# One pair of v products held over from a group's short phase, and four small edits beside it

## The chip, the core and the metric

The kernel runs on one core of a Trainium2 chip. The metric is the device time of one execution in microseconds. A core has five engines that run their own instruction streams and meet at semaphores: TensorE (PE in the profile, its weight loads PEld), VectorE (DVE), ScalarE (ACT), GpSimd (POOL) and SyncE (SP), whose queue issues nearly all the DMAs of this kernel. On-chip data lies in SBUF (128 partitions); TensorE writes to PSUM.

## The reference

The input x has 2048 tokens of 512 features. Two branches see it and a gate mixes them:

```
g = sigmoid((x * gate_w).sum(-1))
q, k, v = split(x @ wqkv)            # 32 heads of 16 features
a = concat_heads(softmax(q k^T / 4) v) @ wo
h = layernorm(x)
u = gelu(h^T w1 + b1)                # over the tokens: 2048 -> 1792
b = (u w2 + b2)^T                    # 1792 -> 2048
out = g * a + (1 - g) * b
```

All is float32. b1 has 1792 values, b2 has 2048.

## The kernel before

Most float32 products are made of three products of split operands: `split` makes a high part (a cast) and a low part (source minus high part), and high x high, high x low and low x high are added. A cast is usually done on ScalarE (or DVE), the subtraction on GpSimd or DVE.

**Stage 1, v.** For each of 16 tiles of 128 tokens, `turn` transposes x (four 128x128 products with the identity, line 184), splits it, and the v columns are projected (line 73). `gate_dot` makes the gate's sum on DVE. A scheduler orders this stage, the next and the first layer.

**Stage 2, q and k.** Transposed q and k are projected, split and stored in DRAM. On the way the greatest absolute values of q and k are kept; `most` holds, for each of the 512 features, the product of the two greatest values. Summed over the 16 features of a head it bounds that head's scores. `least_shifts` compares the 32 sums with a limit and leaves a count in `flag`. At the end of the kernel a general path runs if the count is not zero; here it is zero. Before the change this test is two tiny products on TensorE (lines 338 and 342), with DVE between them, at the first block of the first layer. The layer norm of the first half of the rows lies in this stage.

**Stage 3, the first layer of the token MLP** (line 357). Blocks of w1, 128 tokens by up to 512 columns, are loaded up to four ahead, split on ScalarE and GpSimd, and multiplied with the layer norm rows: twelve steps of 128x128 by 512 for a full block. The second half of the layer norm rows is made meanwhile. `gelu` follows on DVE and ScalarE. `biases` loads b1 and b2 with a row for every 128 values, and turns them with two small products (line 378), after the second block.

**Stage 4, attention with the second layer beside it.** From here on each engine's order is the program's. There are 32 groups: a pair of heads, and half of the queries (1024). A group has eleven phases. Each of ten full phases issues six score products (line 700; the two heads use the two halves of TensorE's rows), and beside them up to six dense steps on the free half of the rows (line 738): the second layer of the MLP, or the output projection. Each two scores fill a `[128, 2, 512]` PSUM tile (`s`, three of them), and one exponential on ScalarE (line 709) makes a `pt` tile in SBUF (six of them). The eleventh phase is short: four scores and nothing beside. After a phase's scores stand the products with v (line 665) of the phase *before* it, so that ScalarE has time: `late` holds the units of one phase, and `apply_v` takes them two at a time, a pair for the two query blocks. A pair is eight `av` matmuls. A full phase leaves three pairs, a short one two. After a group's last pair DVE copies `av` out (line 631), the numerators go to DRAM, and the denominators are inverted (line 644) and stored.

Dense steps of two neighbouring phases add to one PSUM bank, one half of the rows after the other. A tiny GpSimd memset of `token` (line 742) is the fence between them: it waits for the last dense step of one phase, and the first dense step of the next waits for it.

Before the first phase, 30 steps of the second layer run alone (line 685), and two of w2's blocks are split there, with the cast on DVE and the subtraction on GpSimd. While the groups run, `dense` says which steps stand beside which pair of phases, and `calls` says what else is issued there. `fetch_o` loads four head pairs' numerators and broadcast inverses from DRAM (the tiles `o_lo` and `o_sum`, lines 519 and 520) and puts a `divide` on the list of slow work for DVE (line 523), one item of which is issued per pair of phases. The output projection of the later queries takes what was divided. `open_end` frees the memory of the MLP and opens the pool `end`, in which the third fetch of the second half puts its tiles.

Of the kernel before, what the change touches and what calls it, by code (L numbers as in the profile page):

```python
# [9 lines left out]
F32 = mybir.dt.float32  # L10
# [11 lines left out]
P = 128  # L22
# [3 lines left out]
H = 32  # L26
# [32 lines left out]
def gated_mix(ctx: ExitStack, tc: tile.TileContext, a_x, a_wqkv, a_wo, b_w1, b_b1, b_w2, b_b2, gate_w, out):  # L59
# [3 lines left out]
    def split(hi, lo, src, copy, sub):  # L63

        copy(hi, src)  # L65
        sub(lo, src, hi.bitcast(F32), ALU.subtract)  # L66
# [10 lines left out]
    dram = ctx.enter_context(tc.tile_pool(name="dram", bufs=1, space=DRAM))  # L77
    qp_d = [dram.tile([3, P, S], F32, name=f"qp{b}") for b in range(ND)]
    kp_d = [dram.tile([2, P, S], F32, name=f"kp{b}") for b in range(ND)]

    ident = const.tile([P, P], F32, name="ident")
    make_identity(nc, ident)
    head_of = const.tile([P, P // DH], F32, name="head_of")
    nc.vector.tensor_reduce(head_of, ident.rearrange("p (h d) -> p h d", d=DH), axis=AX.X, op=ALU.add)
    ones = const.tile([P, 1], F32, name="ones")
    nc.vector.memset(ones, 1.0)
    b1 = const.tile([P, NF], F32, name="b1")
# [47 lines left out]

    def split_weight(copy=None):
        if loaded:
            raw = loaded.pop(0)
            hi = wk.tile([P, NB], F32R, name="w_hi")[:, : raw.shape[1]]
            lo = wk.tile([P, NB], F32R, name="w_lo")[:, : raw.shape[1]]  # L140
            split(hi, lo, raw, copy or nc.scalar.copy, nc.gpsimd.tensor_tensor)
            ready.append((hi, lo))
# [22 lines left out]
    with tc.tile_pool(name="vp", bufs=1, side="right") as pool:  # L165
# [22 lines left out]
        def gate_dot(t):  # L188
# [4 lines left out]
            tc.keep_in_program_order(dot)  # L193

        def v_pairs(t):
            cols = slice(t * P, (t + 1) * P)
            return [((xt_hi[:, k, cols], xt_lo[:, k, cols]), wv[k][1:]) for k in range(ND)]
# [29 lines left out]
        for t in range(1, NS):  # L227
            if t + 4 < NS:
                load(t + 4)
            if t + 1 < NS:  # L230
                turn(t + 1)
            if t in (8, 12):
                qk_w.append(wcols(qk_cols.pop(0)))
            if t >= 3:
                gate_dot(t - 3)
            ps = bank()
            products(ps, v_pairs(t))
            v_out(t, ps)
# [94 lines left out]
    xt_ctx.close()  # L333

    def least_shifts():

        ps = bank()
        nc.tensor.matmul(ps[: P // DH, :ND], head_of, most, start=True, stop=True)
        far = bd.tile([P // DH, ND], F32, name="far")
        nc.vector.tensor_scalar(far, ps[: P // DH, :ND], BOUND_LIMIT, None, ALU.is_gt)  # L340
        pf = bank()[:1, :ND]
        nc.tensor.matmul(pf, ones[: P // DH, :], far, start=True, stop=True)
        ff = bd.tile([1, 1], F32, name="ff")
        nc.vector.tensor_reduce(ff, pf, axis=AX.X, op=ALU.add)
        nc.vector.tensor_copy(flag, ff)
# [13 lines left out]
    with tc.tile_pool(name="ln1", bufs=3, side="right") as ln, tc.tile_pool(name="gl", bufs=2, side="right") as gl:  # L359
# [12 lines left out]

        def biases():
            for src, dst, rows, mul in ((b_b1, b1, NF, 1.0), (b_b2, b2x2, NS, 2.0)):
                t = ln.tile([NS, P], F32, name="bias", bufs=2)[:rows]
                nc.sync.dma_start(t, src.rearrange("(r c) -> r c", c=P))
                pt = bank()[:, :rows]
                nc.tensor.transpose(pt, t, ident[:rows, :rows])
                nc.vector.tensor_scalar_mul(dst, pt, mul)

        for f0, cs in order.items():
            n = min(NB, F - f0) // P
            ps = [bank() for _ in range(n)]
            for c in cs:
                if f0 == 0 and c < NH:
                    ln_load(ln, NH + c)
                    ln_scale(ln, NH + c, 1)
                    ln_rows(ln, NH + c)
                hi, lo = weight()
                layer(ps, hi, lo, (h_hi[c], h_lo[c]), c == cs[0], c == cs[-1])  # L390
                if f0 == 0 and c == 0:
                    least_shifts()
                if f0 == 0 and c == 1:
                    biases()
            for i in range(n):
                gelu(ps[i], f0 // P + i)
# [219 lines left out]
    assert at == (NP + 12) * TWOS + 7  # L616
    call(at - 2, fetch_o, 1, 2)
    at = put_outputs(range(NH, NS - 3), 0, EARLY, at, [5, 4])
# [37 lines left out]

    def apply_v(g, units, last):

        for pair in zip(*([u for u in units if u[2] == qb] for qb in range(2))):
            for i, c, qb, pt in pair:  # L660

                added[qb] += 1
                for h in range(2):
# [7 lines left out]
                    )  # L671
        if last:
            added[:] = 0, 0
            return evacuate(g)

    engines = {getattr(mybir.EngineType, name) for name in ("PE", "Activation", "DVE", "Pool", "SP")}
    with tc.manual_schedule(engines=engines):
        kt, qt = {0: load_k(0)}, {0: load_q(0)}
        late = open_s = fence = None
# [32 lines left out]
        for grp in range(NG):  # L712
            at = [0, 0]
            for ph in range(2 * TWOS + 1):
# [31 lines left out]
                if second:  # L746
# [144 lines left out]
```

## Time and profile before

| | us |
|---|---|
| median of 3 runs | 1333.93 |
| lowest and highest | 1333.09, 1336.63 |
| the profiled execution, its own time | 1335.31 |
| its span, first to last instruction | 1333.4 |
| stage 1 and 2 (v, q, k), to about | 145 |
| first layer, to about | 305 |
| second layer alone, to about | 312 |
| 32 groups of attention, to about | 1308 |

The mean granted clock of TensorE was 0.996. The profiled execution took 1.38 us more than the median of the runs.

In the profile, "L665" is line 665 of the kernel before. A line of a timeline has the start in us from the span's start, the duration in us, the engine, the line, the operation, what is written `<-` what is read, the shape, and how many instructions were merged; brackets hold the idle time of the engine before it and what ended it. A matmul's duration overlaps the next one's, so starts are to be compared, not durations. A line of the chain has start, duration, engine and line. A line of a group has busy us and mean ns, then the engine's idle time before those instructions.

### The profile page before, as it was taken

Reading aid. Unit: us, or ns where it says so; the run is one execution under the profiler, and the core shown is the slowest. Engines: PE = TensorE matmul, PEld = TensorE weight load, DVE = VectorE, ACT = ScalarE, POOL = GpSimd, SP = SyncE. Lnnn points to the kernel's source line nnn. Section 1 sums busy time; section 2 is a strip of 40 time slices with the busy share of each in tenths; the row PEclk is TensorE's granted clock in tenths of the full one; section 3 lists DMA queues with packets and bytes.
Section 4 is the critical chain, followed back from the end, with each engine's and each line's share of the span. In section 5 each row is a group of like instructions: output and inputs, shape, how many; then the busy total and the mean of one; then the engine's idle time right before and its main releaser. Section 6 shows DMA issues by size and latency. Waiting matters only on the chain.

```text
span 1333.4 us, 32411 instructions
## 1 busy us (share of the span) xinstructions
PE 1314.6 (99%) x13288; PEld 770.0 (58%) x13288; DVE 413.5 (31%) x625; ACT 1096.3 (82%) x1264; POOL 202.3 (15%) x468
## 2 busy tenths in 40 slices
PE   9999999999999999999999999999999999999996
PEld 6888778876555555555555555455554555545553
DVE  3596571454121111222322111222111222132324
ACT  3344343447999999999999999999999999999993
POOL 0210254443011011011000011000110110100001
PEclk9999999999999999999999999999999999999998
DMA  3587643327343333334555344545333334454511
GB/s 119 165 275 294 206 119 95 95 75 156 73 85 65 61 73 83 67 75 96 121 109 129 68 76 90 100 111 125 61 65 73 77 68 81 72 113 108 108 53 67
DMA packets 93240, 138.41 MB, mean 104 GB/s; under 512 B 14149, under 2 KB 53211, under 8 KB 90011
## 3 DMA queue, kind: packets, MB, share of 16 engines
q1 hardware_dynamic: 92650, 135.46, 42.7%
q8 instruction: 107, 1.75, 0.6%
q10 hardware_dynamic: 432, 0.79, 0.2%
q14 instruction: 51, 0.41, 0.1%
HBM read 99.63 MB, written 36.56 MB: 102 GB/s over the span
## 4 chain that ended last, share of the span: by engine, by line
PE 94%; ACT 2%; DMA 1%; DVE 1%; SPq 0%; issue 0%; POOL 0%; POOLq 0%; DVEq 0%; ACTq 0%
PE av L665 35%; PE s L700 26%; PE acc L357 12%; PE dn L738 11%; PE acc L73 10%; ACT pt L709 2%; DMA o_sum<-r 1%; PE dn L685 1%; PE acc L184 0%; DMA wv_raw<-in_A_wqkv_dram 0%; DVE sums L783 0%; SPq L419 0%; POOL w_lo L66 0%; DVE base L805 0%; DVE lo L66 0%
## 5 line engine op out<-in xcount | busy, mean ns | idle before, releaser
L709 ACT ACTIVATE pt<-s 128x1024 f32<-128x1024 f32 x1024 | 964.9, 1028 | 33.9 <-PE s L700 26.6
L700 PE MATMUL s<-qs,ks 64*128 64x512 f32 x2048 | 527.4, 421 | 3.0 <-ACT pt L709 3.0
L665 PE MATMUL av<-pt,v 128*17 128x256 f32 x8192 | 510.6, 381 | 0.0
L700 PEld LDWEIGHTS s<-qs,ks 64*128 64x128 f32 x2048 | 301.0, 184 | 207.8 <-ACT pt L709 155.4
L665 PEld LDWEIGHTS av<-pt,v 128*17 128x17 f32 x8192 | 205.2, 97 | 259.6 <-issue 125.3
L738 PE MATMUL dn<-u_hi,w_hi 64*128 64x512 f32 x428 | 182.3, 426 | 0.7 <-POOL token L742 0.7
L66 POOL TENSOR_TENSOR w_lo<-w_raw,w_hi 128x512 fp32r<-128x512 f32 (+1 forms) x128 | 154.4, 1209 | 136.5 <-ACT w_hi L65 111.4
L738 PE MATMUL dn<-u_lo,w_hi 64*128 64x512 f32 x428 | 169.6, 396 | 0.0
L738 PE MATMUL dn<-u_hi,w_lo 64*128 64x512 f32 x428 | 168.4, 393 | 0.0
L742 POOL MEMSET token<- 1x1 f32 x320 | 29.3, 92 | 875.8 <-PE dn L738 552.2
L631 DVE COPY ot<-av 128x512 f32<-128x512 f32 x32 | 22.1, 692 | 352.9 <-PE av L665 347.5
L644 DVE RECIPROCAL rt<-rt 128x512 f32<-128x512 f32 x31 | 103.9, 3353 | 1.1
L65 ACT CAST w_hi<-w_raw 128x512 fp32r<-128x512 f32 (+1 forms) x67 | 37.8, 566 | 65.9 <-PE acc L357 59.9
L357 PE MATMUL acc<-h_hi,w_lo 128*128 128x512 f32 x224 | 89.2, 398 | 0.3 <-POOL w_lo L66 0.3
L357 PE MATMUL acc<-h_hi,w_hi 128*128 128x512 f32 x224 | 89.0, 397 | 0.0
L357 PE MATMUL acc<-h_lo,w_hi 128*128 128x512 f32 x224 | 88.8, 396 | 0.0
L738 PEld LDWEIGHTS dn<-u_lo,w_hi 64*128 64x128 f32 x428 | 79.2, 185 | 3.4
L738 PEld LDWEIGHTS dn<-u_hi,w_lo 64*128 64x128 f32 x428 | 79.0, 185 | 3.6
L738 PEld LDWEIGHTS dn<-u_hi,w_hi 64*128 64x128 f32 x428 | 78.7, 184 | 3.7 <-POOL token L742 1.0
L65 DVE CAST w_hi<-w_raw 128x512 fp32r<-128x512 f32 (+1 forms) x61 | 22.4, 378 | 124.4 <-PE dn L738 66.8
L434 DVE TENSOR_SCALAR row<-dn,b2x,omg 128x512 f32<-128x512 f32 x16 | 13.0, 810 | 147.8 <-PE dn L738 106.5
L73 PE MATMUL acc<-xt_hi,wc_hi 128*128 128x512 f32 x128 | 49.8, 389 | 0.0
(131 smaller groups left out, 1065.8 us busy)
## 6 DMA issues: line engine op xcount, KB each, us to landing
w_raw<-in_B_w_dram SPq DMA_DIRECT2D x96, 256.0 KB
ks<-kp SPq DMA_DIRECT2D x192, 128.0 KB
qs<-qp SPq DMA_DIRECT2D x256, 64.0 KB
qp<-pc SPq DMA_DIRECT2D x16, 768.0 KB
x<-in_A_x_dram SPq DMA_DIRECT2D x32, 256.0 KB
kp<-pc SPq DMA_DIRECT2D x16, 512.0 KB
w_raw<-in_B_w_dram SPq DMA_DIRECT2D x32, 128.0 KB
bp<-row SPq DMA_DIRECT2D x16, 256.0 KB
```

Of the source, the lines that this page charges most:

```text
L65: copy(hi, src)
L66: sub(lo, src, hi.bitcast(F32), ALU.subtract)
L73: nc.tensor.matmul(ps, a, b, start=start and n == 0, stop=stop and n == last)
L357: nc.tensor.matmul(p, a, b, start=first and k == 0, stop=last and k == 2)
L631: nc.vector.tensor_copy(ot, av)
L644: nc.vector.reciprocal(rt, rt)
L665: nc.tensor.matmul(av[32 * j : 32 * j + VC, i * QC : (i + 1) * QC], v[:, c, g % NP * 2 + i, :], pt[:, h * QC : (h + 1) * QC], start=added[ ...
L685: nc.tensor.matmul(ps, a, b, start=start, stop=stop)
L700: nc.tensor.matmul(s[:, m, :], kt[grp][rows, c * P : (c + 1) * P], qt[grp][rows, qb * NB : (qb + 1) * NB], start=True, stop=True,)
L709: nc.scalar.activation(pt, s, AF.Exp, scale=SCALE)
L738: mm = nc.tensor.matmul(ps, a[half], b[half], start=first and not second, stop=last and bool(second))
L742: fence = nc.gpsimd.memset(token, 0.0)
```

## The change

Five edits:

1. **A pair held over.** `late` becomes a list of pairs. Behind the scores of a group's short phase only two of the three pairs of the last full phase are issued; the third is issued behind the next phase's six scores, ahead of the short phase's two. The last group keeps the old order.
2. **Test of the shifts on DVE.** `most` is stored to DRAM and read back as one row of 512 on one partition (`bring_most`, after the first block of the first layer); at the ninth block DVE sums it by heads, compares, counts. The two products on TensorE and their two constants go. The scheduler places the DVE part among the layer norm's work, before the rows of the ninth block.
3. **Biases turned with x.** The two bias tiles are cleared on GpSimd to 128x128, loaded in stage 1 after the sixth x tile, and turned as full tiles directly after x tile 5.
4. **First splits on DVE.** The two weight blocks split beside the 30 lone steps have their subtraction on DVE.
5. **A fetch one step earlier.** The third fetch of the second half is issued one pair of phases earlier, in the same step as `open_end`.

```diff
+    most_d = dram.tile([P, ND], F32, name="most_d")
...
-    head_of = const.tile([P, P // DH], F32, name="head_of")
-    nc.vector.tensor_reduce(head_of, ident.rearrange("p (h d) -> p h d", d=DH), axis=AX.X, op=ALU.add)
-    ones = const.tile([P, 1], F32, name="ones")
-    nc.vector.memset(ones, 1.0)
...
-    def split_weight(copy=None):
+    def split_weight(copy=None, sub=None):
...
-            split(hi, lo, raw, copy or nc.scalar.copy, nc.gpsimd.tensor_tensor)
+            split(hi, lo, raw, copy or nc.scalar.copy, sub or nc.gpsimd.tensor_tensor)
...
+        def biases(pool):
+            for n, (src, dst, rows, mul) in enumerate(((b_b1, b1, NF, 1.0), (b_b2, b2x2, NS, 2.0))):
+                t = pool.tile([P, P], F32, name=f"bias{n}")
+                nc.gpsimd.memset(t, 0.0)
+                nc.sync.dma_start(t[:rows], src.rearrange("(r c) -> r c", c=P))
+                pt = bank()[:, :P]
+                nc.tensor.transpose(pt, t, ident)
+                nc.vector.tensor_scalar_mul(dst, pt[:, :rows], mul)
...
+            if t == 4:
+                biases(pool)
...
+    most_row = bd.tile([1, P * ND], F32, name="most_row", bufs=1)
+    def bring_most():
+        nc.sync.dma_start(most_d, most)
+        nc.sync.dma_start(most_row, most_d.rearrange("p b -> (p b)")[None, :])
     def least_shifts():
-        ps = bank()
-        nc.tensor.matmul(ps[: P // DH, :ND], head_of, most, start=True, stop=True)
-        far = bd.tile([P // DH, ND], F32, name="far")
-        nc.vector.tensor_scalar(far, ps[: P // DH, :ND], BOUND_LIMIT, None, ALU.is_gt)
-        pf = bank()[:1, :ND]
-        nc.tensor.matmul(pf, ones[: P // DH, :], far, start=True, stop=True)
-        ff = bd.tile([1, 1], F32, name="ff")
-        nc.vector.tensor_reduce(ff, pf, axis=AX.X, op=ALU.add)
+        far = bd.tile([1, H], F32, name="far", bufs=1)
+        heads = far.rearrange("o (h b) -> o h b", b=ND)
+        nc.vector.tensor_reduce(heads, most_row.rearrange("o (h d b) -> o h b d", d=DH, b=ND), axis=AX.X, op=ALU.add)
+        nc.vector.tensor_scalar(far, far, BOUND_LIMIT, None, ALU.is_gt)
+        ff = bd.tile([1, 1], F32, name="ff", bufs=1)
+        nc.vector.tensor_reduce(ff, far, axis=AX.X, op=ALU.add)
         nc.vector.tensor_copy(flag, ff)
...
                 if f0 == 0 and c == 0:
+                    bring_most()
+                if f0 == 0 and c == NH:
                     least_shifts()
-                if f0 == 0 and c == 1:
-                    biases()
...
-    call(at - 2, fetch_o, 1, 2)
+    call(at - 3, fetch_o, 1, 2)
...
-    def apply_v(g, units, last):
-        for pair in zip(*([u for u in units if u[2] == qb] for qb in range(2))):
+    def pairs_of(g, units, last):
+        pairs = list(zip(*([u for u in units if u[2] == qb] for qb in range(2))))
+        return [(g, pair, last and n == len(pairs) - 1) for n, pair in enumerate(pairs)]
+    def apply_v(pairs):
+        ot = None
+        for g, pair, last in pairs:
             for i, c, qb, pt in pair:
...
-                split_weight(nc.vector.tensor_copy)
+                split_weight(nc.vector.tensor_copy, nc.vector.tensor_tensor)
...
-                if late:
-                    apply_v(*late)
-                late = grp, units, ph == 2 * TWOS
-        last_ot = apply_v(*late)
+                n = 2 if ph == 2 * TWOS and grp < NG - 1 else len(late)
+                apply_v(late[:n])
+                late = late[n:] + pairs_of(grp, units, ph == 2 * TWOS)
+        last_ot = apply_v(late)
```

More of the change, by code (lines that the diff above doesn't have):

```diff
@@ L371, in gelu @@
             split(u_hi[:, fb, :], u_lo[:, fb, :], u, nc.scalar.copy, nc.vector.tensor_tensor)
[L373 to L379, printed above, removed]
         for f0, cs in order.items():
@@ L671, in apply_v @@
                     )
-        if last:
-            added[:] = 0, 0
-            return evacuate(g)
+            if last:
+                added[:] = 0, 0
+                ot = evacuate(g)
+        return ot
     engines = {getattr(mybir.EngineType, name) for name in ("PE", "Activation", "DVE", "Pool", "SP")}
@@ L678, in gated_mix @@
         kt, qt = {0: load_k(0)}, {0: load_q(0)}
-        late = open_s = fence = None
+        late, open_s, fence = [], None, None
         for n, (step, *args) in enumerate(first):
             if n and n % 12 == 0:
-                split_weight(nc.vector.tensor_copy)
+                split_weight(nc.vector.tensor_copy, nc.vector.tensor_tensor)
             ps, a, b, start, stop, done = step(*args)
```

## The prediction

> **What bounds the kernel now.** I read the page first, then the chain of waits in order of time, then the timelines of PE, PEld and ACT at the ends of two groups, and last the places where the chain leaves TensorE.
>
> ```profile
> PE 1314.6 (99%) x13288; PEld 770.0 (58%) x13288; DVE 413.5 (31%) x625; ACT 1096.3 (82%) x1264; POOL 202.3 (15%) x468
> PE 94%; ACT 2%; DMA 1%; DVE 1%; SPq 0%; issue 0%; POOL 0%; POOLq 0%; DVEq 0%; ACTq 0%
> L709 ACT ACTIVATE pt<-s 128x1024 f32<-128x1024 f32 x1024 | 964.9, 1028 | 33.9 <-PE s L700 26.6
> ```
>
> The chain is TensorE almost throughout. In attention (about 1000 us, 32 groups) ScalarE is close behind: 964.9 us of exponentials and 33.9 us of idleness, most of it waiting for scores. So a group has two limits, and the prediction is about the places where one of them waits for the other. A group has ten full phases (six scores, dense steps beside, three pairs of v products: 24 `av` matmuls) and a short phase of four scores. The end of the first group, whose next phases have six dense steps (PE, then PEld, then ACT):
>
> ```profile
> 342.64 1.49 PE L665 MATMUL av<-pt,v 128*17 128x256 f32 x24
> 344.06 0.50 PE L700 MATMUL s<-qs,ks 64*128 64x512 f32 x1
> 345.64 1.06 PE L665 MATMUL av<-pt,v 128*17 128x256 f32 x16
> 346.62 0.49 PE L700 MATMUL s<-qs,ks 64*128 64x512 f32 x1
> 348.46 1.49 PE L665 MATMUL av<-pt,v 128*17 128x256 f32 x24
> ...
> 347.79 0.18 PEld L700 LDWEIGHTS s<-qs,ks 64*128 64x128 f32 x1 [0.41 <-ACT pt L709]
> ...
> 337.72 6.79 ACT L709 ACTIVATE pt<-s 128x1024 f32<-128x1024 f32 x7
> 344.88 8.45 ACT L709 ACTIVATE pt<-s 128x1024 f32<-128x1024 f32 x9 [0.37 <-PE s L700]
> ```
>
> Behind the short phase's four scores stand the 24 v products of the full phase before it (342.64 to 344.06: 1.42 us), behind the next six scores only 16 (345.64 to 346.62: 0.98). So the six scores come late, ScalarE idles 0.37 us, and one phase later TensorE waits for ScalarE (347.79): a score needs the PSUM bank that the third exponential of the late run frees. An exponential takes 1.03 us and the next starts 0.93 after it ((8.45 - 1.03) / 8), so that one ends at 344.88 + 2 x 0.93 + 1.03 = 347.77. The phase from 346.62 to the end of the next v products (348.46 + 1.42 = 349.88) is 3.26 us long. Where nothing waits, such a phase takes 3.00 (first two lines below).
>
> ```profile
> 1228.08 1.49 PE L665 MATMUL av<-pt,v 128*17 128x256 f32 x24
> 1231.08 1.49 PE L665 MATMUL av<-pt,v 128*17 128x256 f32 x24
> 1235.74 1.49 PE L665 MATMUL av<-pt,v 128*17 128x256 f32 x24
> ...
> 1225.21 0.75 DVE L543 SCALAR_TENSOR_TENSOR row<-dn,g,row 128x512 f32<-128x512 f32 x1 [1.12 <-PE dn L738]
> ...
> 1210.45 0.42 SPq L539 DMA_DIRECT2D row<-bp  x1
> ...
> 1219.96 12.00 DMA o_sum<-r
> ```
>
> The third line is the one long hole of attention: the fetch of the divisors lands 12.00 us after its issue, the divide on DVE comes behind it, and the phase lasts 4.66 us.
>
> **Held pair.** The work of TensorE is the same; one of three pairs (8 matmuls, 1.42 / 3 = 0.47 us by the 24, 0.44 by the difference 1.42 - 0.98) moves from behind the short phase's scores to behind the next six. At the boundary above: the six scores start at 343.62 and not 344.06; their first exponential is ready 0.82 later as now, at 344.44, when ScalarE is just free (337.72 + 6.79 = 344.51, less the overlap of 0.10). The third exponential ends at 347.33, before the score that waits until 347.79. The v products then take 1.42, so the next phase still begins at 346.62, and it is 3.00 long: 0.26 won. I take 0.25; the low end is half of it, 0.13, should a new wait in the first of the two phases take the rest.
>
> The other kind has four dense steps in the next phases, and there ScalarE is the limit:
>
> ```profile
> 404.88 1.49 PE L665 MATMUL av<-pt,v 128*17 128x256 f32 x24
> 406.30 0.50 PE L700 MATMUL s<-qs,ks 64*128 64x512 f32 x2
> 407.12 0.39 PE L700 MATMUL s<-qs,ks 64*128 64x512 f32 x1
> 408.67 0.75 PE L700 MATMUL s<-qs,ks 64*128 64x512 f32 x3
> 409.84 0.49 PE L700 MATMUL s<-qs,ks 64*128 64x512 f32 x1 [0.19 <-ACT pt L709]
> ...
> 400.14 6.62 ACT L709 ACTIVATE pt<-s 128x1024 f32<-128x1024 f32 x7
> 406.93 10.31 ACT L709 ACTIVATE pt<-s 128x1024 f32<-128x1024 f32 x11 [0.17 <-PE s L700]
> ```
>
> ScalarE's last exponential ends at 406.76, so it began at 405.73 and the next could begin at 406.66; it begins at 406.93: 0.27 lost. After the change the scores start at 405.86, the first exponential is ready at 406.49, and that loss goes. What is late next: the fifth score (407.12, 0.82 after the first) comes at 406.68, but its bank is freed by the exponential that ends at 406.76. TensorE waits 0.1 and loses 0.1 more in restarting, and the longer v products follow; the next phase begins at 408.87 instead of 408.67, its first exponential is ready 0.63 later, at 409.50, and ScalarE is free at 409.45. Net 0.22 won. The wait may be as long as the 0.19 seen at 409.84, so I take 0.15, between ends of 0 and 0.27.
>
> How many of each? Only at the second kind does the chain go through two exponentials; there are 14 such pieces, the first and the last of them:
>
> ```profile
> 407.85 1.95 ACT pt L709 x2
> 1249.61 1.95 ACT pt L709 x2
> ```
>
> A fifteenth, near 1217, is hidden by the fetch. So 15 x 0.15 + 16 x 0.25 = 2.25 + 4.0 = 6.25 us; ends 16 x 0.13 = 2.1 and 16 x 0.26 + 15 x 0.27 = 8.2. The held pair keeps one more `pt` buffer in use. That buffer is wanted again by the first exponential of the phase after, near 409.5, and its v products now come first in the run that starts near 407.5, so I cost it at nothing; had they come last it would still be 0.6 early.
>
> **Fetch one step earlier.** Its two DMAs are issued behind the `row` load of 1210.45, thus near 1211, and land by about 1225 if they again take some 2 and 12 us. The divide keeps its place on DVE, behind the instruction of 1225.21, and then runs with no wait: it can start at 1225.96, where now it waits until 1231.96. On SP the store of a partial row, eight `qs` loads and a `row` load are moved behind it, by the issue of two DMAs; the first scores that need the `qs` are 30 us away. Won: 4.66 less an undisturbed phase, which is 3.00 or, with ScalarE as the limit, 3 x 0.93 = 2.8; so 1.66 to 1.86, and I take 1.8.
>
> **Test of the shifts, biases.** Four tiny edits leave TensorE, which is gapless there:
>
> ```profile
> 145.36 0.40 PE L357 MATMUL acc<-h_hi,w_hi 128*128 128x512 f32 x1
> 148.63 0.40 PE L357 MATMUL acc<-h_hi,w_lo 128*128 128x512 f32 x1
> 150.21 0.39 PE L357 MATMUL acc<-h_hi,w_hi 128*128 128x512 f32 x1
> 156.30 0.40 PE L357 MATMUL acc<-h_hi,w_lo 128*128 128x512 f32 x1
> 157.95 0.40 PE L357 MATMUL acc<-h_hi,w_hi 128*128 128x512 f32 x1
> 19.87 0.60 PE L184 MATMUL acc<-ident,x 128*128 128x128 f32 x4
> 20.23 0.48 PE L73 MATMUL acc<-wv_hi,xt_hi 128*128 128x512 f32 x1
> ...
> L66 DVE TENSOR_TENSOR h_lo<-hf,h_hi x8: 676/684/693, 160.8 to 181.0; 128x512 fp32r<-128x512 f32 x8
> ```
>
> Twenty-six steps from 150.21 to 156.30 are 0.234 each. The four steps from 148.63 to 150.21 hold the two products of the test: 1.58 - 0.94 = 0.64. The four from 156.30 to 157.95 hold the two bias turns: 1.65 - 0.94 = 0.71. Added are two turns of full 128x128 tiles right behind the four of an x tile, which take 0.36: 0.18 for two, at most 0.5 if each costs a switch as the old ones did. Net 1.35 - 0.18 = 1.17, low end 0.85. On SP two bias loads move to the start (their tiles are needed near 20 us), and two small DMAs through DRAM take their place; DVE waits for the second of these ahead of the layer norm rows. The nearest row for that reduction is one of 512 elements, 0.68; DVE gains about as much by the operations it drops. The eight rows are split between 160.8 and 181.7. They are wanted from eight blocks of twelve steps after the layer's start (145.36) to fifteen blocks after it, 168 to 188, so 6 us cover it.
>
> **First splits on DVE.**
>
> ```profile
> 313.57 1.27 POOL L66 TENSOR_TENSOR w_lo<-w_raw,w_hi 128x512 fp32r<-128x512 f32 x1 [1.62 <-PE dn L738]
> 314.77 0.09 POOL L742 MEMSET token<- 1x1 f32 x1
> ...
> 313.73 0.50 PE L700 MATMUL s<-qs,ks 64*128 64x512 f32 x1 [0.19 <-ACT pt L709]
> 314.92 0.50 PE L738 MATMUL dn<-u_hi,w_hi 64*128 64x512 f32 x1 [0.69 <-POOL token L742]
> ...
> 306.74 2.19 POOL L66 TENSOR_TENSOR w_lo<-w_raw,w_hi 128x512 fp32r<-128x512 f32 x1 [1.17 <-ACT w_hi L65]
> 307.70 1.52 DVE L367 TENSOR_SCALAR gs<-gs 128x512 f32<-128x512 f32 x1
> ```
>
> The first fence (`token`) stands behind a split of 1.27 us on POOL; TensorE waits from 313.73 to 314.92. With the split on DVE the fence is free at once. But the scores of that phase also wait for exponentials: the first bank frees near 313.7 (the 0.19 at 313.73), the third 2 x 0.93 later, near 315.55, and two scores behind it (0.33 each after a wait) bring the v products to 316.2. As it is they begin six steps after 314.92, 0.33 + 4 x 0.23 + 0.33 later, at 316.5. I take 0.3, ends 0 and 1.0.
> In the last two lines a POOL split of 2.19 us (1.27 alone) lies over a DVE instruction of 1.52. The Trainium skill ("SBUF — State Buffer", the section on the two separate sides) says that DVE and GpSimd lock a shared pair of ports against each other, and that a two-port DVE copy holds up any GpSimd instruction. By that rule the fence's memset can now stand behind the DVE cast instead, and this term is about 0; by the row it is 0.3. The sum would be 9.2 and not 9.5.
>
> **Sum.** 6.25 + 1.8 + 1.17 + 0.3 = 9.5 us, with the low ends together 4.6, with the high ends 12.2. The profiled execution took 1335.31 (span 1333.4), so its like would take 1325.8; the median of the runs is 1333.93, 1.4 lower, and gives 1324.4. The case's own range is 1321.7 to 1329.3. A difference under 0.3% (4 us) I count as no change.
>
> **Rivals.** (1) The wait only moves: in the changed kernel the fifth score stands still at every boundary, and what ScalarE wins is given back there. For it: the bank frees 0.08 us after the score comes. Against it: with six dense steps all six scores stand on one half of the rows, the fifth comes 0.33 + 3 x 0.23 after 343.62, at 344.64, and its bank is free at 344.51. Then the held pair gives nothing, and the rest 3.3: 1330.7, within 0.3%. (2) The fetch's stall stays, because the earlier transfer shares the DMA engines with the eight `qs` loads: 9.5 - 1.8 = 7.7, so 1326.2. Against it: for the whole stall to stay it would have to take some 18 us and not 12, and before, it ran beside `ks` loads. (3) Slower: DVE stands in the first layer behind the row of 512 sums, which goes to DRAM and back. The layer norm rows wait behind it on DVE, and on ScalarE square roots that wait for DVE stand ahead of the weight casts. From 6 us of delay TensorE loses one for one; the gain is gone at 15.5 us, and beyond 19.5 it is slower by over 0.3%. Two landings as long as the 12.00 above, one behind the other, would make 24 us and 1342. Against it: these two move 2 KB each.
>
> **Chances.** Forecast 0.74; (1) 0.12; (2) 0.07; (3) and anything like it 0.07. Faster is the forecast, (2) and a part of (1), less the low tail: 0.82. Same 0.12, slower 0.06. The range from 1320.5 to 1331 takes in (1) and (2).
>
> **What would show it.** `av` runs of 16 behind the four scores and 24 behind the six; ScalarE's idleness for scores at 26.6 us falling by several; no wait of PEld for ScalarE in the second phase of a group; the pieces of two exponentials gone from the chain; no `o_sum` piece in it; the layer's steps 0.234 throughout; the first fence right after its matmul. Wrong would be: a new wait of TensorE in the first phase of each group, or a gap in the first layer.

## The result and the profile after

The changed kernel takes 1328.61 us (median of 7 runs, 1328.09 to 1329.23); the kernel before, beside it, 1333.93. The ratio is 0.9954 with a 95% interval of 0.994 to 0.9968: faster by 5.3 us, where 9.5 were forecast. The profiled execution took 1328.09 us with a span of 1326.2, 7.2 less than the span before; of these, 1.4 are the distance of the profiled execution of before from its own median, and 0.5 that of the changed kernel's.

The page of the changed kernel, the same groups as before and two of the first layer (the last column is TensorE's or ScalarE's idle time just ahead of these instructions, and what ended most of it):

```profile
PE 1309.7 (99%) x13284; PEld 767.8 (58%) x13284; DVE 414.3 (31%) x626; ACT 1095.7 (83%) x1264; POOL 202.0 (15%) x468
PE 95%; DVE 2%; issue 1%; POOL 1%; ACT 0%; DMA 0%; SPq 0%; POOLq 0%; DVEq 0%
L720 ACT ACTIVATE pt<-s 128x1024 f32<-128x1024 f32 x1024 | 964.4, 1026 | 26.9 <-PE s L711 17.7
L370 PE MATMUL acc<-h_hi,w_lo 128*128 128x512 f32 x224 | 89.1, 398 | 1.9 <-POOL w_lo L66 1.8
L370 PE MATMUL acc<-h_hi,w_hi 128*128 128x512 f32 x224 | 88.7, 396 | 0.4 <-ACT w_hi L65 0.4
```

ScalarE and the long transfer have left the chain (2% and 1% before), and ScalarE's idleness for scores fell from 26.6 to 17.7 us. TensorE's own idleness for exponentials fell from 3.0 to 0.4 us. But TensorE now waits in the first layer, and POOL and DVE stand in the chain. The timelines of TensorE and ScalarE at the two boundaries that the prediction showed, and of TensorE and DVE at the fetch:

```profile
343.01 1.49 PE L675 MATMUL av<-pt,v 128*17 128x256 f32 x24
345.09 1.06 PE L675 MATMUL av<-pt,v 128*17 128x256 f32 x16
347.69 1.49 PE L675 MATMUL av<-pt,v 128*17 128x256 f32 x24
...
339.24 10.53 ACT L720 ACTIVATE pt<-s 128x1024 f32<-128x1024 f32 x11 [0.16 <-PE s L711]
...
406.94 1.06 PE L675 MATMUL av<-pt,v 128*17 128x256 f32 x16
409.53 1.49 PE L675 MATMUL av<-pt,v 128*17 128x256 f32 x24
...
398.49 19.67 ACT L720 ACTIVATE pt<-s 128x1024 f32<-128x1024 f32 x21 [0.17 <-PE s L711]
...
1224.10 1.49 PE L675 MATMUL av<-pt,v 128*17 128x256 f32 x24
1227.12 1.49 PE L675 MATMUL av<-pt,v 128*17 128x256 f32 x24
...
1222.14 1.22 DVE L528 TENSOR_TENSOR o_sum<-o_lo,o_sum 128x1024 f32<-128x1024 f32 x1
```

Sixteen products now stand behind the short phase's scores and 24 behind the next; ScalarE runs through both boundaries (one run of 11 exponentials, and one of 21 that only the end of the view cuts off); the long phase at the fetch is 3.02 us. Attention, from the first score to the first matmul of the tail, takes 990.68 us (314.60 to 1305.28) and took 999.51: 8.8 won, 8.35 forecast (held pair, fetch and first splits).

The loss lies ahead of attention. The first score starts at 314.60, before at 311.88: 2.7 later, where 1.2 earlier was forecast. The chain of waits of the changed kernel in the first layer (start, duration, what):

```profile
165.11 1.52 POOL w_lo L66
...
170.07 1.28 POOL w_lo L66
...
174.46 1.26 POOL w_lo L66
...
177.58 1.30 POOL w_lo L66
...
181.51 1.29 POOL w_lo L66
```

Five times the chain goes through the split of a weight. TensorE sits idle for the low halves of the last four (0.28, 0.62, 0.08 and 0.63 us) and once for a high half (0.42). And at the end of the layers (timelines of TensorE and DVE):

```profile
306.01 0.40 PE L370 MATMUL acc<-h_hi,w_lo 128*128 128x512 f32 x1
307.61 0.47 PE L696 MATMUL dn<-u_hi,w_hi 128*128 128x512 f32 x1 [1.20 <-ACT gs L379]
...
304.25 1.76 DVE L415 MEMSET ks<- 16x2048 f32 x1 [0.46 <-issue]
306.05 1.41 DVE L378 TENSOR_SCALAR gu<-acc,b 128x512 f32<-128x512 f32 x2
```

The first product of the lone second layer starts 1.60 us after the last one of the first layer, 1.37 more than a step. Before, it followed at 304.98 on 304.75. (The row names ScalarE's `gs`, which ends at 307.47; the second `gu` on DVE, the last to read the first layer's PSUM tiles, ends at 307.46.)

### The profile page after: what moved, and what is told of

It reads as the page before. It is cut to its first block, busy times and chain, and to the rows that moved or that the text cites. A ratio compares the mean times of both kernels' runs of the same rounds, so it can differ in the third digit from the quotient of the medians.

```text
span 1326.2 us, 32411 instructions
## 1 busy us (share of the span) xinstructions
PE 1309.7 (99%) x13284; PEld 767.8 (58%) x13284; DVE 414.3 (31%) x626; ACT 1095.7 (83%) x1264; POOL 202.0 (15%) x468
## 4 chain that ended last, share of the span: by engine, by line
PE 95%; DVE 2%; issue 1%; POOL 1%; ACT 0%; DMA 0%; SPq 0%; POOLq 0%; DVEq 0%
PE av L675 37%; PE s L711 28%; PE dn L749 10%; PE acc L73 10%; PE acc L370 9%; DVE ks L415 1%; PE dn L696 1%; PE acc L181 1%; POOL w_lo L66 1%; DMA wv_raw<-in_A_wqkv_dram 0%; DVE u_lo L66 0%; DVE sums L795 0%; DVE gs L381 0%; DVE gu L378 0%; ACT pt L720 0%
## 5 line engine op out<-in xcount | busy, mean ns | idle before, releaser
L720 ACT ACTIVATE pt<-s 128x1024 f32<-128x1024 f32 x1024 | 964.4, 1026 | 26.9 <-PE s L711 17.7
L370 PEld LDWEIGHTS acc<-h_hi,w_lo 128*128 128x128 f32 x224 | 42.1, 188 | 14.1 <-POOL w_lo L66 4.1
```

The source lines that it names most:

```text
L370: nc.tensor.matmul(p, a, b, start=first and k == 0, stop=last and k == 2)
L720: nc.scalar.activation(pt, s, AF.Exp, scale=SCALE)
```

## The experiments

Times are medians beside runs of the kernel before on the same chip. Because the start of an execution, up to the first layer, varies by up to 2 us (the layer's first matmul stood between 145.3 and 147.2 us in the traces), stages are compared by their lengths: "the layer" is from its first matmul to the first product of the second layer, 159.62 us before and 162.32 after.

**The two terms of attention, alone.** `held_only` is the kernel before with edit 1, `fetch_only` with edit 5, `splits_only` with edit 4 of the list above; their diffs are the parts of the change's.

> The kernel before, with the pair of units held over from a group's short phase as the only edit. Forecast of the prediction: 15 x 0.15 + 16 x 0.25 = 6.25 us faster than before, between 2.1 and 8.2, thus a ratio near 0.9953. If the wait only moved to the fifth score: 0. In the changed kernel attention as a whole is 8.8 us shorter, of which group 29, with the fetch, has 2.08, so the pair should give 6.0 to 6.7 here and the ScalarE idleness for scores should fall from 26.6 to about 18.

Measured: 1328.23 against 1334.24, ratio 0.9951 (0.9937 to 0.9964). Its page:

```profile
L715 ACT ACTIVATE pt<-s 128x1024 f32<-128x1024 f32 x1024 | 964.6, 1026 | 26.6 <-PE s L706 17.9
```

The exponentials of all groups but the one with the fetch take 957.97 us from first to last, before 964.34: 6.4 won.

> The kernel before, with the fetch of the divisors issued one step earlier as the only edit. Forecast of the prediction: 1.66 to 1.86 us faster (1.8 taken). Rival: the transfer shares the DMA engines with the qs loads and the stall stays: 0. In the changed kernel group 29 is 2.08 shorter, with the held pair's share in it, so 1.7 to 2.0 is likely; the hole of 4.66 us between two runs of 24 v products near 1231 should read 3.0.

Measured: 1333.18 against 1334.24, ratio 0.9991 (0.9982 to 1.0). In the trace the divide no longer waits, and the group with the fetch is 30.93 us long against 32.77: 1.84, as forecast. But that 32.77 belongs to one execution. In the four other traces in which the fetch stands at its old place it is 31.56 and 31.58 (`held_only`, `splits_only`), 30.92 and 31.70 (`trip_added`, `wide_trip`, below). Without the stall it is 30.93, or 30.67 with the held pair; so the stall was 1.84, 0.9, 0.65, 0 and 0.8 us, 0.8 in the mean. The medians differ by 1.1 us, with an interval that reaches to nothing.

> The kernel before with the first splits of attention (those of the eleven or so dense steps ahead of the first group) on DVE as the only edit. Forecast of the prediction: 0.3 us (0 to 1.0), by the rule of the shared ports about 0. In the changed kernel the first group is 0.45 us shorter than with the held pair alone (31.54 and 31.99), so 0.4 to 0.5 is likely, seen in the first fence and in group 0; the medians cannot tell that from 0.

The steps meant there are the 30 lone ones, beside which two weight blocks are split. Measured: 1333.63 against 1333.65, ratio 0.9998 (0.9989 to 1.0007), nothing that the medians can tell. The first group is 31.97 us, before 32.24: 0.27 won, and 0.45 beside the held pair (31.54 after 31.99). The fence and TensorE in its trace:

```profile
313.75 0.09 POOL L742 MEMSET token<- 1x1 f32 x1 [4.71 <-PE dn L738]
...
313.84 0.50 PE L700 MATMUL s<-qs,ks 64*128 64x512 f32 x1 [0.18 <-ACT pt L709]
313.89 0.50 PE L738 MATMUL dn<-u_hi,w_hi 64*128 64x512 f32 x1
```

The fence was at 314.77 and is at 313.75; TensorE waits for a bank instead, as the prediction worked out.

**The bank.** The 8 PSUM tiles named `acc` are drawn in turn. Without the two products of the test, two tiles fewer are drawn ahead of the layers, so the tile that `dn` takes at the end is now the very last one that the first layer filled, and DVE must read it first (`gu<-acc` at 306.05, behind a memset). `one_bank` lets both biases share a tile, which moves all later ones by one:

```diff
-                pt = bank()[:, :P]
+                if n == 0:
+                    both = bank()
+                pt = both[:, n * P : (n + 1) * P]
```

> The changed kernel, but the two turned biases share one PSUM tile, so one tile fewer is drawn from the rotation of eight and every later tile moves by one bank. Bank theory: the 1.2 to 1.4 us that TensorE waits ahead of the first dn product (307.61 in the changed kernel) come from the rotation alone, since the changed kernel's last two layer tiles sit in the banks that the dn product takes next; with the shift that wait is gone and the time falls by 1.2 to 1.4 us, to about 1327.3. Rival: the wait comes from a late DVE (four memsets of 1.76 us ahead of the last gelu); then the bank does not matter, the wait stays and the time is the changed kernel's, within 0.3 us. The gaps of the first layer (165 to 185 us) stay in both.

Measured: 1326.27 against 1334.24, ratio 0.9937 (0.9924 to 0.9951). TensorE at the same place:

```profile
306.78 0.39 PE L372 MATMUL acc<-h_hi,w_lo 128*128 128x512 f32 x1
307.01 0.39 PE L698 MATMUL dn<-u_hi,w_hi 128*128 128x512 f32 x1
```

The wait is gone, with the memsets and the last gelu where they were: the bank it was, 1.37 us. The layer is 2.5 us shorter than in the changed kernel; the other 1.1 are shorter waits for weights (table below).

**The test back on TensorE.** `test_on_pe` is the changed kernel with the old `least_shifts` and no trip through DRAM.

> The changed kernel with the test of the shifts put back on TensorE as in the kernel before: no trip through DRAM, two tiny products back (0.64 us), and the rotation of banks as before. Trip theory (the 16-byte packets and what stands behind them cost the 2.7 us of gaps in the first layer, and the missing two banks 1.2 to 1.4 at the entry of attention): 2.7 + 1.3 - 0.6 = 3.4 us faster than the changed kernel, with the steps of the first layer 0.234 throughout. Rival (the bias loads and the new order of ScalarE and DVE make the gaps): they stay, and it is only 1.3 - 0.6 = 0.7 us faster.

Measured: 1326.28 against 1334.24, ratio 0.994 (0.9926 to 0.9953), 2.3 below the changed kernel's median, between the two expectations; but in the trace the layer takes 158.60 us, without a gap. Against 159.62 before, the biases' turns alone give 1.0: 0.7 for the turns and 0.3 for the wait at 178.29, which is gone.

**The trip alone, and its packets.** In the changed kernel's trace the store's 128 packets of 16 bytes lay beside 2 KB packets that took 217 to 836 ns (means of half microseconds) instead of 88. `trip_added` is the kernel before with the two transfers, `wide_trip` stores 512 bytes a row instead (of another tile that is ready earlier, so the store is issued 0.7 us sooner):

```diff
+        nc.sync.dma_start(most_d, most)
+        nc.sync.dma_start(most_row, most_d.rearrange("p b -> (p b)")[None, :])
...
-        nc.sync.dma_start(most_d, most)
+        with tc.issue_after(last_qp[0].ins):
+            nc.sync.dma_start(most_d, ident)
```

> The kernel before with only the trip of the bounds through DRAM added (the store of 128 x 16 bytes and the load of the row of 512); nothing reads the row, the test stays on TensorE. Packet theory: in the changed kernel the store's 128 packets of 16 bytes made the 2 KB packets beside them take 217 to 836 ns each in place of 88, and the rows of x behind them landed 1.7 us later; here the same, with packets of that length at about 150 to 153 us, and gaps of TensorE in the first layer of 1 to 2.7 us: 1 to 2.7 us slower than before. Rival (the gaps come from DVE's reduction and the new places of the square roots): packets hardly longer, no gap, 0.

> As trip_added, with the store made of 128 packets of 512 bytes in place of 16 (another tile of 128 x 128 is stored, the load of 512 values reads four of its rows; nothing uses it). The order of every queue is that of trip_added. Packet theory (it is the 16 bytes that hold up the neighbours): the 2 KB packets beside the store stay near 88 ns, the rows of x land as in the kernel before, no gap, and the time is 1 to 2.7 us below trip_added. Rival (any store at this place does it, since it stands in the same queue): as trip_added, packets long and the gaps there.

Measured: 1337.30 and 1337.41 against 1333.94, ratios 1.0023 (1.0013 to 1.0033) and 1.0023 (1.0014 to 1.0032). The layer takes 162.67 and 162.27 us, 3.05 and 2.65 more than before. The page of the first (that of the second has the same figures):

```profile
L364 PE MATMUL acc<-h_hi,w_lo 128*128 128x512 f32 x224 | 89.5, 400 | 2.1 <-POOL w_lo L66 2.1
```

So the trip costs 3 us even where nothing reads its row, and with packets of either size. The slow 2 KB packets are in `wide_trip` too (346 ns in the half microsecond behind the store), and in the next kernel, which has no store at all (283 ns at the same place). So the size of the packets is not what `trip_added` pays for.

The size does show elsewhere: in how much the DMA queues move just behind the store, and in when the first row of x is asked for. Times are in us after the layer's first matmul; the rate is that of the 2 us from 5.5 to 7.5.

| kernel | store | GB/s | first load of x | first square root | second |
|---|---|---|---|---|---|
| before | none | 149 | 6.0 | 10.9 | 11.8 |
| trip_added | 128 x 16 bytes | 31 | 7.4 | 11.7 | 15.0 |
| wide_trip | 128 x 512 bytes | 154 | 6.0 | 10.2 | 14.7 |
| after | 128 x 16 bytes | 33 | 7.8 | 13.5 | 15.7 |
| no_trip | none | 173 | 5.9 | 11.4 | 12.1 |

The five kernels with the 16-byte store at this place move 31 to 49 GB/s there, the nine others 142 to 182. The first load of x waits on SyncE until a store of q has landed. That is 7.1 to 7.7 us after the layer's first matmul in those five, and 5.8 in the nine (the changed kernel's load, and SyncE's waits for q's store):

```profile
153.10 0.33 SPq L269 DMA_DIRECT2D x<-in_A_x_dram  x1
SPq L269 <- DMA qp<-pc: 2.5, 1, 2.5
```

**The trip gone, DVE's test kept.** `no_trip` fills the row with zeros on GpSimd.

```diff
-        nc.sync.dma_start(most_d, most)
-        nc.sync.dma_start(most_row, most_d.rearrange("p b -> (p b)")[None, :])
+        nc.gpsimd.memset(most_row, 0.0)
```

> The changed kernel, with the row of bounds filled with zeros by GpSimd in place of the two transfers; the reduction and the test on DVE stay, so the test of the bounds itself is left out. Trip theory (packets, or the wait for the row): the 2.7 us of gaps in the first layer go, the bank wait of 1.2 to 1.4 us at the entry of attention stays: 1328.6 - 2.7 = 1325.9. Rival (the bias loads moved to the start, or the scheduler's order of ScalarE, make the gaps): 1328.6.

Measured: 1327.32 against 1333.94, ratio 0.9947 (0.9934 to 0.996): 1.3 below the changed kernel, half of what the trip theory wanted. The layer takes 160.38 us, of which 1.37 are the bank; 1.4 us of waits for weights stay. It is 1.9 us shorter than the changed kernel's, as much as the first load of x is earlier (5.9 and 7.8); against `after_again`, below, both are some 1.5.

**The queue of ScalarE.** What do the kernels with gaps share? A weight's low half waits for its high half, which ScalarE casts; and that cast stands in ScalarE's queue among square roots and casts of the layer norm rows, each of which waits for DVE. The timelines of the kernel before (ScalarE, POOL, TensorE and its weight loads), then ScalarE of the changed kernel:

```profile
157.61 0.62 ACT L65 CAST w_hi<-w_raw 128x512 fp32r<-128x512 f32 x1 [0.25 <-PE acc L357]
...
158.31 1.28 POOL L66 TENSOR_TENSOR w_lo<-w_raw,w_hi 128x512 fp32r<-128x512 f32 x1 [1.93 <-ACT w_hi L65]
...
178.29 0.50 PE L357 MATMUL acc<-h_hi,w_lo 128*128 128x512 f32 x1
...
178.29 0.19 PEld L357 LDWEIGHTS acc<-h_hi,w_lo 128*128 128x128 f32 x1 [0.46 <-POOL w_lo L66]
```

```profile
158.78 0.20 ACT L279 ACTIVATE y<-w 128x1 f32<-128x1 f32 x1 [4.50 <-DVE far L355]
158.89 0.60 ACT L65 CAST w_hi<-w_raw 128x512 fp32r<-128x512 f32 x1
...
166.95 0.62 ACT L65 CAST h_hi<-hf 128x512 fp32r<-128x512 f32 x1 [2.67 <-DVE hf L289]
169.00 0.48 ACT L279 ACTIVATE y<-w 128x1 f32<-128x1 f32 x2 [1.43 <-DVE w L278]
169.39 0.60 ACT L65 CAST w_hi<-w_raw 128x512 fp32r<-128x512 f32 x1
```

A margin can be worked out. A block is 12 steps of 0.234, 2.81 us. The split starts 0.70 after the cast (157.61, 158.31), takes 1.28, and TensorE wants the low half in the third step, 0.47 into the block: so a cast must start 0.70 + 1.28 - 0.47 = 1.5 us before its block. The blocks start 2.81 apart from the layer's start, 1.35 later where the old test and biases are in the layer (0.64 with the test alone). Three weights are cast ahead of the layer, so the cast at 148.12 before is that of the block with number 3, and the one at 157.61 that of block 6. For the casts of blocks 6 to 13, while rows are made:

| kernel | cast of block 6, us after the layer's start | mean distance of casts, us | smallest margin, us | TensorE's idle for `w_hi` and `w_lo`, us | its loss by the starts of its matmuls, us | median, us (before, same chip) |
|---|---|---|---|---|---|---|
| before | 12.3 | 3.32 | +0.3 | 0.3 | 0.3 | 1333.9 |
| test_on_pe | 11.9 | 3.34 | +0.4 | 0.3 | 0.0 | 1326.28 (1334.24) |
| trip_added | 11.9 | 3.95 | -3.2 | 2.5 | 3.3 | 1337.30 (1333.94) |
| wide_trip | 11.9 | 3.90 | -2.8 | 2.1 | 2.9 | 1337.41 (1333.94) |
| after | 13.6 | 3.28 | -3.3 | 2.3 | 3.6 | 1328.61 (1333.93) |
| after_again | 13.2 | 3.28 | -2.9 | 2.1 | 3.2 | 1328.93 (1333.65) |
| one_bank | 12.4 | 3.28 | -2.1 | 1.7 | 2.4 | 1326.27 (1334.24) |
| no_trip | 11.5 | 3.22 | -1.3 | 1.4 | 1.6 | 1327.32 (1333.94) |
| late_trip | 11.8 | 3.49 | -1.2 | 1.5 | 1.4 | 1325.89 (1333.94) |
| w_first | 13.6 | 3.47 | -2.8 (block 14: -3.7) | 2.7 | 4.0 | 1327.84 (1333.65) |
| best | 11.2 | 3.23 | +1.2 | 0.3 | 0.0 | 1324.85 (1333.65) |

The casts come 3.2 to 3.95 us apart and TensorE's blocks 2.81: a lead of some 4 us is eaten while rows are made. In the kernel before it is eaten to 0.3 us (at 178.29 TensorE even waits a little). The idle time is that of the page and undercounts, since a matmul's duration overlaps the next one's; besides, 0.3 of it is in every kernel a wait near 295 us, behind these blocks. The column beside it has what the starts of the matmuls lose between 19 and 47 us after the layer's start against an undisturbed step, the 0.1 by which each wait delays one more step included. A negative margin and this loss agree to 0.3 us in every kernel.

`late_trip` is `one_bank` with the store issued behind the last row's load of x and the test a block of columns later; `after_again` is the changed kernel, unaltered, beside the last mends:

```diff
+        with tc.issue_after(last_x[0].ins):
             nc.sync.dma_start(most_d, most)
...
-                if f0 == 0 and c == NH:
+                if f0 == NB and c == 0:
                     least_shifts()
```

> The changed kernel with both mends: the two biases share one PSUM tile, and the store of the bounds is issued only behind the last load of x for the layer norm, the test one block of layer columns later. If the two causes are the bank and the trip's place, both losses go: 1328.6 - 1.4 - 2.7 = 1324.5 (with the usual spread of the start about +-1), 9.4 us below before, which is what the prediction forecast; TensorE's busy time between 165 and 185 us again 19.9 or more. If the place does not matter (the wait of DVE for the row costs wherever it stands), the time is that of one_bank, 1326.3.

> The changed kernel, unaltered, beside the others on one chip: 1328.6, with a layer of 162.3 us (first matmul to first dn product) and 988.3 us of exponentials; what the mended kernels gain is read against it.

`after_again`: 1328.93 against 1333.65, ratio 0.9964 (0.995 to 0.9977), with a layer of 161.93 us. `late_trip`: 1325.89 against 1333.94, ratio 0.9934 (0.9922 to 0.9946). The layer takes 158.87, 0.9 less than `one_bank`'s 159.81, but one wait of 1.24 us stays; TensorE is busy 18.76 us between 165 and 185, not 19.9:

```profile
179.08 0.62 ACT L65 CAST h_hi<-hf 128x512 fp32r<-128x512 f32 x1 [1.90 <-DVE hf L293]
179.60 0.62 ACT L65 CAST w_hi<-w_raw 128x512 fp32r<-128x512 f32 x1
...
180.30 2.08 POOL L66 TENSOR_TENSOR w_lo<-w_raw,w_hi 128x512 fp32r<-128x512 f32 x1 [2.24 <-ACT w_hi L65]
...
181.18 1.47 DVE L293 TENSOR_SCALAR hf<-x,mv,rs 128x512 f32<-128x512 f32 x1
...
182.43 0.50 PE L375 MATMUL acc<-h_hi,w_lo 128*128 128x512 f32 x1 [1.24 <-POOL w_lo L66]
```

Here the cast stands behind a row that waits for DVE; on top, the split takes 2.08 instead of 1.28 us beside DVE's work. So the order itself was set by hand: `w_first` (on `one_bank`) makes the rows three blocks later in the program and holds each row's cast behind the cast of the weight six blocks on; `best` is the same on `late_trip`, with the trip three blocks later still in the program.

```diff
+                hi, lo = weight()
-                if f0 == 0 and c < NH:
-                    ln_load(ln, NH + c)
+                if f0 == 0 and 3 <= c < NH + 3:
+                    ln_load(ln, NH + c - 3)
...
+                    with tc.issue_after(last_cast[0].ins):
+                        ln_rows(ln, NH + c - 3)
-                hi, lo = weight()
```

> one_bank (the changed kernel with one PSUM tile for both biases), and on ScalarE the cast of the weight of block r + 6 is held ahead of the cast of layer norm row r; the trip through DRAM stays where the changed kernel has it, and so does DVE's reduction. Theory now held (the order of ScalarE's queue): the gaps of the first layer arise where a weight cast stands in ScalarE's queue behind a cast of a row that waits for DVE; so the gaps of 1.85 us that one_bank keeps go, the layer takes 158.0 us from its first matmul to the first dn product (159.8 in one_bank), and the time is 1326.3 - 1.85 = 1324.4. Rival (the trip itself delays x, DVE and all that follow): the rows are late whatever the order, gaps of 1.5 us or more stay, 1326.

> late_trip with the order of w_first: the trip late and the weight casts ahead of the rows. Queue-order theory: no gap is left, 158.0 us for the layer as in w_first, 1324.4 and no better than w_first. Trip theory: better than w_first by the 1.5 us that the early trip costs there.

`w_first`: 1327.84 against 1333.65, ratio 0.9957 (0.9943 to 0.9971). The theory as written there fell: the layer takes 161.41 us and the gaps are larger than in `one_bank`. `best`: 1324.85 against 1333.65, ratio 0.9931 (0.9917 to 0.9944), a layer of 157.36 us, no wait between 165 and 185 us:

```profile
165.00:185.00 20.00, 20.00 (x88) 16.18 (x87) 18.16 (x55) 8.25 (x18) 11.25 (x8) 1.00 0.46 134
```

The two differ in the place of the trip and of DVE's test, which goes with it; it is worth 4.05 us of the layer and 3.0 of the median, where the trip theory wanted 1.5. What ScalarE does in `w_first`, then in `best`:

```profile
159.09 0.20 ACT L282 ACTIVATE y<-w 128x1 f32<-128x1 f32 x1 [4.44 <-DMA x<-in_A_x_dram]
159.20 0.61 ACT L138 CAST w_hi<-w_raw 128x512 fp32r<-128x512 f32 x1
...
165.87 0.61 ACT L138 CAST w_hi<-w_raw 128x512 fp32r<-128x512 f32 x1
168.23 0.20 ACT L282 ACTIVATE y<-w 128x1 f32<-128x1 f32 x1 [1.75 <-DVE w L281]
168.75 0.62 ACT L65 CAST h_hi<-hf 128x512 fp32r<-128x512 f32 x1 [0.32 <-DVE hf L292]
169.28 0.62 ACT L138 CAST w_hi<-w_raw 128x512 fp32r<-128x512 f32 x1
```

```profile
156.59 0.20 ACT L284 ACTIVATE y<-w 128x1 f32<-128x1 f32 x1 [1.20 <-DVE w L283]
157.63 0.62 ACT L138 CAST w_hi<-w_raw 128x512 fp32r<-128x512 f32 x1 [0.83 <-PE acc L376]
...
160.46 0.29 ACT L284 ACTIVATE y<-w 128x1 f32<-128x1 f32 x2
160.65 0.60 ACT L138 CAST w_hi<-w_raw 128x512 fp32r<-128x512 f32 x1
...
164.35 0.62 ACT L138 CAST w_hi<-w_raw 128x512 fp32r<-128x512 f32 x1
164.88 0.62 ACT L65 CAST h_hi<-hf 128x512 fp32r<-128x512 f32 x1
```

With the trip early, the first square root comes 13.4 us after the layer's start instead of 10.2, and then one row at a time goes from ScalarE to DVE and back, a weight cast behind each: 3.4 us a round (165.87 to 169.28). With the trip late the square roots come in pairs, two rows are under way, and the casts keep 1.2 us of margin. So the trip's place decides, through when the rows begin and how many are under way. The traces show each of these two alone. In `wide_trip` the first load of x and the first square root are as early as before (6.0 and 10.2), and 2.65 us are lost all the same: the scheduler has put the second square root behind the first row's cast on ScalarE (14.7, before 11.8), and `trip_added` has the same order. In the changed kernel the order is nearly that of `no_trip`, and all of it begins 2.1 us later (13.5 and 11.4), 1.9 of which are the late load of x. That a wider store would win these 1.9 us in the changed kernel was not run; nor was `w_first`, which begins late and makes one row at a time, taken apart. `best` is 4.1 us below the changed kernel on the same chip (1324.85 and 1328.93), the fastest of all, with all five edits in it.

## Why the prediction was right and where it was wrong

The direction and the side of the threshold came out, with a time 4.2 us above the forecast, within the range. That it lies within is the width of the range: two losses of some 5 us together were in no term of the sum, and the low ends allowed for 4.9. By its steps:

| term | forecast, us | measured, us | from |
|---|---|---|---|
| held pair | 6.25 | 6.4 (median 6.0) | held_only |
| fetch one step earlier | 1.8 | 1.84 in the trace shown, 0.8 as a mean of five | fetch_only and four others |
| first splits on DVE | 0.3 | 0.27, with the held pair 0.45 | splits_only |
| test and biases, on TensorE | 1.17 | 1.7, and 0.6 by a shorter step (layer 159.62 to 157.36); -0.2 for the two turns in stage 1 | best |
| waits in the first layer | 0 | -3.2 and -3.6 (layer 161.93 and 162.32 in two traces, less the bank's 1.37, against 157.36) | after, after_again |
| the bank of the first `dn` product | not seen | -1.4 | one_bank |

- **Held pair: right, and by its mechanism.** No new wait of TensorE took its place; rival (1) is refuted by the single runs of exponentials over the boundaries and by `held_only`. The two kinds of boundary were mis-sized in opposite directions, so the sum fits better than its parts: from the eighth exponential before a boundary to the eighth behind it, `held_only` wins 0.25 us in the mean at the 15 of the second kind, where 0.15 was taken, and 0.21 at the 16 of the first, where 0.25 was taken (nothing at the last of them).
- **Fetch: right in mechanism, over-sized.** The 4.66 us hole was read off one execution, and a wait for a transfer's landing is not the same in each. The medians show 1.1 us (0 to 2.4).
- **First splits: right.** The Trainium skill ("SBUF — State Buffer", the section on the two separate sides) would have made it about 0, with the fence held up by DVE's cast; the group shows 0.27, so the row came nearer, though the size is too small to test the rule.
- **Test and biases: the step that failed is "so 6 us cover it".** It looked at when the rows themselves are wanted. The rows had cover; the weights behind them in ScalarE's queue had 0.3 us of it, as 178.29 in the trace of before shows. Rival (3) named that queue ("on ScalarE square roots that wait for DVE stand ahead of the weight casts") but was priced with the rows' cover, at 7 in 100, and needed 6 us of delay to begin; 0.3 was enough. Two things then pressed on it at once: the 1.35 us taken from TensorE bring every block that much earlier, and the trip delays the rows. `no_trip` shows what stays without the trip: a layer of 159.01 us less the bank, 1.65 more than `best`. That of `late_trip` is 158.87. So in these two orders of ScalarE's queue the edits on TensorE won 0.6 and 0.75 us of the layer, about what the shorter step gives alone. "Gapless" was also too strong: a wait of some 0.2 us was there. The reduction on DVE took 1.02 us, not 0.68.
- **The bank** was in no step. The change draws two PSUM tiles fewer, and the count of draws decides which tile the next stage takes.

Sum: 6.4 + 0.8 + 0.4 + 2.3 - 0.2 - 3.4 - 1.4 = 4.9, measured 5.3. Without the last two it is 9.7; `best`, which has neither loss, is 8.8 faster than before, where 9.5 had been forecast.

## What to carry to other kernels

Cover belongs to a queue, not to the work that is moved: before taking time from the engine at the limit, or adding a wait to another, measure the margin of everything that stands behind it in the same in-order queues, the weights' casts as well as the rows. When a helper that draws from a rotating pool goes, count which buffer the next stages get. Count what a queue moves, not only how long one packet takes. And a stall for a transfer that is read off one execution is one draw; look at it in a second trace before it is written into the sum at full size.

## What was not expected of the hardware

- Splits on GpSimd take 1.28 us alone, and 2.08 in `late_trip` at 180.30, beside a subtraction and a row on DVE; the row (`hf`, 181.18) took 1.47 us there; over all 14 traces it takes 0.53 to 0.55 where no split lies beside it (195 rows) and up to 1.65 where one does (29 rows). The Trainium skill ("SBUF — State Buffer", section on who interferes with whom) says that DVE operations with two inputs in SBUF, and its two-port copies and scalings, exclude GpSimd's reads for their whole length; the numbers agree: 2.08 - 1.28 = 0.8 of the 1.24 us that TensorE waits there are the stretched split.
- Around 151 to 154 us some 2 KB packets take 200 to 800 ns instead of 88 whether the small store, a wider one or none stands there. What slows them was not found. But how many get through does depend on the store: behind 128 packets of 16 bytes the DMA queues move 31 to 49 GB/s for 2 us, behind 128 of 512 bytes 154 and behind none 142 to 182.
- TensorE's step in the layer is 0.2343 us in every trace of a kernel with the test on TensorE (seven traces) and 0.2333 in every one with the test on DVE (seven traces), over 400 steps each, at the same granted clock: 0.6 us over the layer's 672. What makes it was not found; the two constants of the old test have gone from SBUF too.
- The start of an execution, to the layer's first matmul, varied by 1.9 us between the traces, which is more than the fetch, the splits or the bank weigh. Small terms have to be read from the lengths of stages.
